# Gram products of a delta-rule attention: two batches in one matmul of 64 columns by 128, and the key block copied in four pieces

## The chip, the cores and the metric

The kernel runs on one core of one Trainium2 chip. A core has engines with queues of their own, in order: TensorE (PE; its weight loads are listed apart as PEld), VectorE (DVE), ScalarE (ACT), GpSimd (POOL) and SyncE (SP), which here only issues transfers. They wait for each other by semaphores. The metric is the device time of one execution in microseconds; the time before is the median of three executions.

## The reference

The input goes through three layers: a delta-rule attention (4 batches, 8 heads, 768 positions, 48 dimensions), a mixture of experts over the 3072 tokens, and a second, soft mixture. The change is in the first:

```python
k_n = k / (np.linalg.norm(k, axis=-1, keepdims=True) + 1e-06)
state = np.zeros((B, H, D, D), dtype=np.float32)
for t in range(S):
    kt, vt, bt = (k_n[:, :, t], v[:, :, t], beta[:, :, t, None])
    y[:, :, t] = np.einsum('bhd,bhde->bhe', q[:, :, t], state)
    v_old = np.einsum('bhde,bhd->bhe', state, kt)
    state = state + bt[:, :, :, None] * np.einsum('bhd,bhe->bhde', kt, vt - v_old)
```

## The kernel before

The 768 positions are cut into 24 steps of 32 positions, and four steps make a slab, of which there are six. Within a step the recurrence is solved with small matrices: the products of the 32 keys with each other (the Gram block K, 32 by 32 for each batch and head), those of the keys with the 32 queries (A, of which only the strictly later queries count), and a triangular inverse T made from K. All of a step's units lie on 128 partitions: partition 32b + i is batch b, position i; the eight heads lie along the free dimension.

`G(t, hh, lo, hi)` (line 188) computes the Gram products of step t for one head of each pair (hh is 0 or 1; p counts the four pairs). For each p and each batch b, one matmul takes the 32 keys as stationary operand (48 rows by 32 columns) and the 32 keys and 32 queries, or one of both (lo, hi), as the moving one. The output of batch b goes to partitions 32b to 32b + 31, so the four batches use four different groups of 32 columns of the array. That is 16 matmuls per call. Each of the two values of hh has one PSUM bank, Gp[0] or Gp[1] (tiles g).

`E(t, hh, lo, hi)` (line 194) empties the bank. ScalarE copies the K half into the slab's tile GK (line 203). VectorE multiplies the A half by the constant mask am into the tile A (line 208): there A has two places side by side for two neighbouring batches, and the mask is zero in the place of the other one. Two neighbouring batches then go through one matmul of 64 rows where A is used (`AU`, line 412). The next call on the same bank has to wait for both readers.

`main` (line 442) has three parts.

1. The start: eight calls of G and E for the K halves of steps 0 to 3, as soon as the keys land. Then VectorE takes the norms of slab 0 (`norms`, with the transpose of GK, line 223) and builds its inverse in 31 operations (`t_ops`, lines 291 to 323). Behind the fourth and each later one of these stands one call: first the eight A halves of steps 0 to 3, then ten calls of both halves, for steps 4 to 8.
2. The loop over 24 steps. A table ORDER sets the order of a step's parts on all engines: KSa, Ub, V, E1, G0, L, Sb, Ua, AUb, E0, KSb, Sa, QS, Ca, T, AUa, G1. KS (line 358), U (380), Sm (395), QS (367) and AU (412) are the matmuls of the recurrence, for two halves a and b of the heads; ScalarE moves their results on: rs (361), uz and un (382, 383) and sbd (404). G0 and G1 are the calls for step t + 9, so they run in the steps 0 to 14 only, two in each. E0 follows G0 in the same step, E1 follows G1 in the next. T (598) and L (607) begin the expert routing, and in some steps ranks are made and rows sent to the experts' buffer by indirect transfers of GpSimd (716). `advance` spreads VectorE's operations for the next slab's inverse over the step.
3. Behind the loop come the experts and the second mixture. They use neither G nor E.

The keys and queries come from the host turned (48 dimensions on partitions 0 to 47 and 64 to 111 for hh 0 and 1), in the free order batch, pair, position (`layouts`, line 1515; `load_kq`, line 167).

Of the kernel before, what the change touches and what calls it, by code (L numbers as in the profile page):

```python
# [21 lines left out]
NP, NCH, NST, NSL = 4, 12, 24, 6  # L22
# [31 lines left out]
def const_array():  # L54
    a = np.zeros((128, NCONST), np.float32)

    def put(k, v):
        lo, hi = CONST[k]
        a[:, lo:hi] = v

    p = np.arange(128)
    put("idn", np.eye(128))
    i = np.arange(32)[None, :]
    par = p[:, None] // 32 % 2 == np.arange(2)[None, :]
    put("par", par)
    put("lo", np.tril(np.ones((8, 8))).reshape(1, 64))
    put("am", (par[:, :, None] & (i > (p % 32)[:, None])[:, None, :]).reshape(128, 64))
    put("ebase", (np.arange(32) % 8 * ESTR)[None, :])
    put("desc", np.arange(8, 0, -1)[None, :])
    put("tri", p[:, None] < p[None, :])  # L70
    put("iota", np.arange(GT)[None, :])
    put("rep", (p % 32)[:, None] == (p % 32)[None, :])
    put("sel", np.stack([(p % 32) // 4 == p // 32, (p % 32) // 4 == 4 + p // 32], axis=1))
    put("tok", (p // 32 * 768 + p % 32)[:, None] + 32 * np.arange(NST)[None, :])
    g = np.array(GTS)
    put("step", GT * np.arange(NOV)[None, :])
    put("tie", np.arange(1, NE)[None, :] / -16.0)
    put("place", np.arange(1, NE)[None, :])
    put("cap", NG * g[None, :])
    put("gcap", (p // 32)[:, None] * g[None, :])  # L80
    put("grp", (p // 32)[:, None] == np.arange(4)[None, :])
    return a
# [39 lines left out]
class Attention:  # L122
# [5 lines left out]
    def __init__(s, tc, ctx, pctx, kqb, scratch, kq, kz, kv, bt, cst, route):  # L128
        s.tc = tc
        nc = s.nc = tc.nc  # L130
        s.kq, s.kz, s.kv, s.bt = kq, kz, kv, bt
        s.route = route
        e = ctx.enter_context
        s.kvp = e(tc.tile_pool(name="akv", bufs=1))
        s.st = e(tc.tile_pool(name="astat", bufs=1))
        s.wk = e(tc.tile_pool(name="awork", bufs=2))
        s.ps = pctx.enter_context(tc.tile_pool(name="apsum", bufs=1, space=PSUM))
        s.kqb, s.scratch, s.vd = kqb, scratch, {}
        s.kvb = [s.kvp.tile([128, 2, 2, 384], F32, name=f"kv{j}") for j in range(3)]
        s.beta = s.st.tile([128, NSL, 32], F32, name="beta")  # L140
        s.lo, s.am, s.par = cst("lo").rearrange("q (i j) -> q i j", i=8), cst("am").rearrange("q (s i) -> q s i", s=2), cst("par")
        s.zero = s.st.tile([128, 128], F32, name="zero")
        s.mk = s.st.tile([128, 1], F32, name="mk")
        s.Sbd = [[s.st.tile([128, 4, 2, 2, 48], F32, name=f"sbd{x}{j}") for j in range(2)] for x in range(2)]
        s.Uz = [s.st.tile([128, 2, 4, 48], F32, name=f"uz{x}") for x in range(2)]
        s.Un = [s.st.tile([128, 4, 48], F32, name=f"un{x}") for x in range(2)]
        s.RS = [s.st.tile([128, 4, 48], F32, name=f"rs{x}") for x in range(2)]
        s.T = s.st.tile([128, 32, 32], F32, name="T")
        bank = lambda name: s.ps.tile([128, 512], F32, name=name)
        s.Gp = [bank(f"g{hh}") for hh in range(2)]  # L150
        s.Sp = s.ps.tile([128, 2, 512], F32, name="sp")
        s.Wp = [bank(f"w{x}") for x in range(2)]
        s.Yp, s.Pp = bank("y"), bank("p")
        s.W = [w[:, 0:192].rearrange("q (h d) -> q h d", h=4) for w in s.Wp]
        s.Y = s.Yp[:, 0:384].rearrange("q (h d) -> q h d", h=8)
        s.kqt, s.kvt, s.GK, s.A, s.GT, s.TD, s.Tt, s.nN, s.nn = ({} for _ in range(9))
        s.spans = list(SPANS[1:])
        s.got = {}
# [8 lines left out]
    def load_kq(s, c, parts=(0, 1), after=None):  # L167
        if c >= NCH:
            return None
        t = s.kqb[c % 7].rearrange("q (s a x) -> q s a x", s=2, a=2)  # L170
        for j in range(2):
            s.kqt[2 * c + j] = t[:, j].rearrange("q a (b p i) -> q a b p i", b=4, p=4)
        for k in parts:
            i = s.load(t[:, :, k], (s.kz, s.kq)[k][c].rearrange("q (s x) -> q s x", s=2), after)
        return i
# [7 lines left out]


    def gram(s, hh):
        return s.Gp[hh][:, 0:256].rearrange("q (p a i) -> q p a i", p=4, a=2)

    def G(s, t, hh, lo=0, hi=2):
        k = s.kqt[t][64 * hh:64 * hh + 48]
        for p in range(4):  # L190
            for b in range(4):
                s.nc.tensor.matmul(s.gram(hh)[32 * b:32 * b + 32, p, lo:hi], k[:, 0, b, p], k[:, lo:hi, b, p], start=True, stop=True)  # L192

    def E(s, t, hh, lo=0, hi=2):
        v = s.nc.vector
        g = s.gram(hh)
        if lo == 0:
            if t // 4 not in s.GK:
                s.GK[t // 4] = s.wk.tile([128, 32, 32], F32, name="GK", bufs=3)
                s.got[t // 4] = 0  # L200
            s.got[t // 4] += 1
            u = (t % 4) * 8 + 4 * hh
            s.nc.scalar.copy(out=s.GK[t // 4][:, u:u + 4], in_=g[:, :, 0])
        if hi == 2:
            if t not in s.A:
                s.A[t] = s.wk.tile([128, 8, 2, 32], F32, name="A", bufs=AH + 3)
            full = [128, 4, 2, 32]
            v.tensor_tensor(out=s.A[t][:, 4 * hh:4 * hh + 4], in0=g[:, :, 1].unsqueeze(2).to_broadcast(full),  # L208
                            in1=s.am.unsqueeze(1).to_broadcast(full), op=ALU.mult)


# [560 lines left out]
class Experts:  # L772
# [140 lines left out]
    def bank(s, name="aux"):  # L913
        return s.ps.tile([128, 512], F32, name="aux", bufs=3) if name == "aux" else s.ps.tile(
            [128, CAP], F32, name=name, **(dict(bufs=2) if name == "h" else {}))
# [286 lines left out]
    def more(s, e, lo, i):  # L1202
# [57 lines left out]
        v.tensor_scalar(out=nm, in0=gm, scalar1=-1.0, scalar2=None, op0=ALU.mult)  # L1260
        sc.activation(out=corr, in_=m, func=AF.Exp, bias=nm)
        sc.activation(out=E, in_=P[0:32, 0:GT], func=AF.Exp, bias=nm)
        v.tensor_reduce(out=rs, in_=E, axis=AX.X, op=ALU.add)
        v.scalar_tensor_tensor(out=sm, in0=sm, scalar=corr, in1=rs, op0=ALU.mult, op1=ALU.add)
        v.tensor_copy(out=m, in_=gm)
        P = aux()
        nc.tensor.transpose(P[0:GT, 0:32], E, idn[0:32, 0:32])
        En = s.wk.tile([GT, 128], F32, name="En")
        v.tensor_copy(out=En[:, 0:32], in_=P[0:GT, 0:32])
# [244 lines left out]

def layouts(q, k, v, beta, moe_w_gate, moe_w_output_gate, moe_w1, moe_w2, moe2_phi, moe2_w1, moe2_w2):
    def turned(a):
        z = np.zeros((NCH, 2, 64, 2, 4, NP, 32), np.float32)
        z[:, :, :48] = a.reshape(4, NP, 2, NCH, 2, 32, 48).transpose(3, 2, 6, 4, 0, 1, 5)
        return z.reshape(NCH, 128, 1024)

    def natural(a):
        return a.reshape(4, 8, NCH, 2, 32, 48).transpose(2, 0, 4, 3, 1, 5).reshape(NCH, 128, 2, 384)

    kq, kz = turned(q), turned(k)

    z = kz.reshape(NCH, 2, 64, 2, 4, NP, 32)
    for i in range(32):
        z[:, i // 16, 48 + i % 16, :, :, :, i] = -1.0
    kv = np.stack([natural(k), natural(v)], axis=3)
    bt = beta.reshape(4, NP, 2, NSL, 4, 32).transpose(0, 4, 2, 1, 3, 5).reshape(128, NSL, 32)  # L1530
    wgo = np.concatenate([moe_w_gate, moe_w_output_gate], axis=1).reshape(3, 128, 16).transpose(1, 0, 2)
    w1 = moe_w1.reshape(8, 3, 128, 8, 128).transpose(0, 3, 2, 1, 4).reshape(8, 8, 128, 384)
    w = np.concatenate([w1, moe_w2.reshape(8, 8, 128, 384)], axis=-1)
    phi = moe2_phi.reshape(3, 128, 32).transpose(1, 0, 2)
    a = moe2_w1.reshape(2, 4, 3, 128, 2, 512).transpose(0, 4, 2, 3, 1, 5).reshape(12, 128, 2048)
    b = moe2_w2.reshape(2, 4, 8, 128, 384).transpose(3, 0, 2, 1, 4).reshape(128, 64, 384)
    w2 = np.zeros((len(PIECES), 128, 2048), np.float32)
    w2[:12] = a
    q = 12
    for lo, n, units in COLS:  # L1540
        for i, k in enumerate(units):
            u = sum(units[:i])
            w2[q, :, :PIECES[q]] = b[:, u:u + k, lo:lo + n].reshape(128, -1)
            q += 1
    return dict(kq=kq, kz=kz, kv=kv, bt=bt, wgo=wgo, w=w, phi=phi, w2=w2, const=const_array())
# [23 lines left out]
```

## Time and profile before

| | us |
|---|---|
| three executions | 605.73 (median), 600.68, 610.77 |
| profiled execution, whole | 608.46 |
| its span, first to last instruction | 606.7 |
| PE busy | 526.8 (87%) |
| DVE busy | 361.7 (60%) |
| ACT busy | 285.9 (47%) |
| POOL busy | 197.8 (33%) |
| G, line 192: PE, busy | 42.9 for 1792 instructions |
| GK copy, line 203: ACT, busy | 13.5 for 48 |

The busy time of an engine is the union of its instructions' times. Matmuls are pipelined, so many short instructions overlap: the 1792 of line 192 have a mean of 243 ns each. Shares over the whole span mix three stages with different limits; the prediction goes by stage. A row of the timeline merges neighbours of one line: start, length, engine, line, operation, names, count, and in brackets how long the engine was idle before it and what ended that.

### The profile page before, as it was taken

The page shows a single profiled execution, that of the slowest core. Times are in us where ns is not written, and L with a number is a line of the kernel's source. Part 1 is how long each engine was busy: PE and PEld are TensorE (multiplying, and loading weights), DVE is VectorE, ACT ScalarE, POOL GpSimd, SP SyncE. Part 2 cuts the span into 40 slices and gives each one's busy share as a digit, 9 for nine tenths or more (in the row PEclk, how much of TensorE's full clock was granted, in tenths as well). Part 3 has the DMA queues.
Part 4 walks back from the last instruction along what each step waited for, and adds up shares of the span by engine and source line. Part 5 has one row for each costly group of instructions (what it writes and reads, how often), then busy time and mean ns, then how long its engine had stood idle before and what let it go on. Part 6 is the DMA issues. An engine that isn't in the chain of part 4 may idle for free.

```text
span 606.7 us, 21501 instructions
## 1 busy us (share of the span) xinstructions
PE 526.8 (87%) x8944; PEld 435.6 (72%) x8945; DVE 361.7 (60%) x1246; ACT 285.9 (47%) x715; POOL 197.8 (33%) x391
## 2 busy tenths in 40 slices
PE   3278869898889768887988999999999999999994
PEld 3255657676666655665887998989999999996353
DVE  1997996597597797002874645555555656554232
ACT  2014446564646646563543544455545555553222
POOL 2111040245354544345303070605343435250400
PEclk9999687787887969797798999999999999998997
DMA  7676884445432346311559877768543544356448
GB/s 227 228 238 181 242 241 152 150 121 174 127 107 72 93 157 210 109 30 66 170 169 377 320 246 233 274 197 296 159 129 99 153 120 129 104 141 241 191 185 244
DMA packets 50347, 107.76 MB, mean 178 GB/s; under 512 B 5928, under 2 KB 28838, under 8 KB 47557
## 3 DMA queue, kind: packets, MB, share of 16 engines
q1 hardware_dynamic: 47189, 100.77, 51.5%
q0 software_dynamic: 2624, 5.16, 2.5%
q8 instruction: 71, 1.16, 0.8%
q10 hardware_dynamic: 432, 0.41, 0.3%
q14 instruction: 31, 0.25, 0.1%
HBM read 86.19 MB, written 20.13 MB: 175 GB/s over the span
## 4 chain that ended last, share of the span: by engine, by line
PE 71%; DVE 12%; issue 5%; ACT 5%; DMA 4%; POOL 1%; another core or an unknown queue 1%; SPq 0%; ACTq 0%; DVEq 0%
PE h L882 6%; PE y L902 6%; PE h L884 6%; PE h L883 6%; PE y L903 5%; PE y L904 5%; PE sp L395 4%; PE y L412 4%; PE w L358 3%; PE w L380 3%; PE g L192 3%; PE y L367 3%; ACT uz L382 2%; PE fa L1358 2%; PE fc L1379 2%
## 5 line engine op out<-in xcount | busy, mean ns | idle before, releaser
L888 DVE SCALAR_TENSOR_TENSOR hTl<-h,hTh 128x224 fp32r<-128x224 f32 (+7 forms) x72 | 38.4, 534 | 84.0 <-ACT hTh L887 83.8
L806 DVE TENSOR_TENSOR w<-kq,w 128x768 fp32r<-128x768 f32 x72 | 71.0, 986 | 15.9 <-ACT w L805 12.0
L882 PE MATMUL h<-xTh,w 128*128 128x224 f32 (+7 forms) x216 | 76.3, 353 | 2.0 <-ACT w L805 1.7
L884 PE MATMUL h<-xTh,w 128*128 128x224 f32 (+7 forms) x216 | 72.8, 337 | 1.5 <-DVE w L806 1.5
L883 PE MATMUL h<-xTl,w 128*128 128x224 f32 (+7 forms) x216 | 72.2, 334 | 1.4 <-DVE xTl L867 1.4
L902 PE MATMUL y<-hTh,w 128*128 128x224 f32 (+7 forms) x216 | 73.4, 340 | 0.0
L903 PE MATMUL y<-hTl,w 128*128 128x224 f32 (+7 forms) x216 | 71.8, 333 | 0.0
L904 PE MATMUL y<-hTh,w 128*128 128x224 f32 (+7 forms) x216 | 71.7, 332 | 0.0
L192 PE MATMUL g<-kq 48*32 48x64 f32 (+1 forms) x1792 | 42.9, 243 | 30.1 <-DVE A L208 15.2
L805 ACT CAST w<-kq 128x768 fp32r<-128x768 f32 x72 | 59.7, 830 | 7.1 <-DMA kq<-in_w_dram 6.9
L887 ACT ACTIVATE hTh<-h 128x224 fp32r<-128x224 f32 (+7 forms) x72 | 34.0, 473 | 61.5 <-PE h L884 61.3
L306 DVE TENSOR_TENSOR Ttmp<-GT,T 128x110 f32<-128x110 f32 (+21 forms) x276 | 60.9, 261 | 0.2
L310 DVE TENSOR_TENSOR T<-T,Ttmp 128x110 f32<-128x110 f32 (+21 forms) x276 | 59.7, 256 | 0.0
L192 PEld LDWEIGHTS g<-kq 48*32 48x32 f32 x1792 | 32.4, 129 | 37.2 <-DVE A L208 18.8
L1117 POOL TENSOR_TENSOR cd<-cd,csm 112x32 f32<-112x32 f32 (+6 forms) x32 | 10.2, 318 | 132.4 <-DVE csm L1115 98.4
L404 ACT COPY sbd<-sp 48x384 f32<-48x384 f32 x92 | 43.7, 475 | 20.1 <-PE sp L395 19.1
L902 PEld LDWEIGHTS y<-hTh,w 128*128 128x128 f32 x216 | 41.7, 193 | 4.9 <-issue 4.4
L882 PEld LDWEIGHTS h<-xTh,w 128*128 128x128 f32 x216 | 41.8, 194 | 4.1 <-ACT w L805 1.8
L382 ACT ACTIVATE uz<-w,csta 128x192 f32<-128x192 f32 x92 | 33.7, 418 | 23.0 <-remote 11.5
L884 PEld LDWEIGHTS h<-xTh,w 128*128 128x128 f32 x216 | 41.9, 194 | 2.7 <-DVE w L806 2.1
L395 PE MATMUL sp<-uz,kv 64*48 64x96 f32 x736 | 32.4, 300 | 13.1 <-ACT uz L382 9.2
L883 PEld LDWEIGHTS h<-xTl,w 128*128 128x128 f32 x216 | 42.0, 195 | 2.0 <-DVE xTl L867 1.6
(289 smaller groups left out, 1034.6 us busy)
## 6 DMA issues: line engine op xcount, KB each, us to landing
kq<-in_w_dram SPq DMA_DIRECT2D x72, 384.0 KB
rb<-in_w_dram SPq DMA_DIRECT2D x12, 1024.0 KB
kv<-in_kv_dram SPq DMA_DIRECT2D x12, 768.0 KB
kq<-in_w_dram SPq DMA_DIRECT2D x7, 1024.0 KB
kq<-in_kz_dram SPq DMA_DIRECT2D x12, 512.0 KB
kq<-in_kq_dram SPq DMA_DIRECT2D x12, 512.0 KB
xb<-none SPq DMA_DIRECT2D x8, 675.5 KB
v<-kv SPq DMA_DIRECT2D x24, 192.0 KB
```

What stands on the lines that cost most here:

```text
L192: s.nc.tensor.matmul(s.gram(hh)[32 * b:32 * b + 32, p, lo:hi], k[:, 0, b, p], k[:, lo:hi, b, p], start=True, stop=True)
L306: v.tensor_tensor(out=t, in0=L[:, j + 1 + a:j + 1 + b, j:j + 1].to_broadcast([128, b - a, j]), in1=T[:, j:j + 1, :j].to_broadcast([128, b ...
L310: v.tensor_tensor(out=x, in0=x, in1=t, op=ALU.add)
L395: nc.tensor.matmul(S[64 * hh:64 * hh + 48, g, :, 2 * x + p], s.kvt[t][64 * g:64 * g + 64, 0, o:o + 48], s.Uz[x][64 * g:64 * g + 64, :, h], ...
L805: s.nc.scalar.copy(out=h, in_=r)
L806: s.nc.vector.tensor_tensor(out=l, in0=r, in1=h.bitcast(F32), op=ALU.subtract)
L882: nc.tensor.matmul(H, a, xh[:, k, lo:hi], start=(k == 0), stop=False)
L883: nc.tensor.matmul(H, a, xl[:, k, lo:hi], start=False, stop=False)
L884: nc.tensor.matmul(H, b, xh[:, k, lo:hi], start=False, stop=(k == 2))
L902: nc.tensor.matmul(Y, a, h, start=(f == 0), stop=False)
L903: nc.tensor.matmul(Y, a, l, start=False, stop=False)
L904: nc.tensor.matmul(Y, b, h, start=False, stop=(f == 7))
```

## The change

Two neighbouring batches go through one matmul: 64 columns of keys as stationary operand (two batches by 32 positions) and 64 keys and 64 queries, or one of both, as the moving one. A call has eight matmuls instead of 16, with outputs on partitions 0 to 63 and 64 to 127. Each result has the products within a batch and those across the two batches; a call fills a whole PSUM bank instead of half of it. For K only the blocks within a batch are wanted, and they lie in different columns for different batches, so ScalarE copies GK in four pieces of 32 partitions instead of one of 128. VectorE's A reads the same number of elements as before: the mask is zero where the batches differ, so it takes both places as they are instead of one block twice. The host's layout of keys and queries is pair, batch, position instead of batch, pair, position; the transfers have the same sizes.

```diff
@@ load_kq
-            s.kqt[2 * c + j] = t[:, j].rearrange("q a (b p i) -> q a b p i", b=4, p=4)
+            s.kqt[2 * c + j] = t[:, j].rearrange("q a (p b i) -> q a b p i", b=4, p=4)
+            s.kqp[2 * c + j] = t[:, j].rearrange("q a (p g x) -> q a p g x", g=2, p=4)
@@ gram, G
-        return s.Gp[hh][:, 0:256].rearrange("q (p a i) -> q p a i", p=4, a=2)
+        return s.Gp[hh].rearrange("q (p a b i) -> q p a b i", p=4, a=2, b=2)
...
-        k = s.kqt[t][64 * hh:64 * hh + 48]
+
+        k = s.kqp[t][64 * hh:64 * hh + 48]
         for p in range(4):
-            for b in range(4):
-                s.nc.tensor.matmul(s.gram(hh)[32 * b:32 * b + 32, p, lo:hi], k[:, 0, b, p], k[:, lo:hi, b, p], start=True, stop=True)
+            for g in range(2):
+                out = s.Gp[hh][64 * g:64 * g + 64].rearrange("q (p a x) -> q p a x", p=4, a=2)[:, p, lo:hi]
+                s.nc.tensor.matmul(out, k[:, 0, p, g], k[:, lo:hi, p, g], start=True, stop=True)
@@ E
-            s.nc.scalar.copy(out=s.GK[t // 4][:, u:u + 4], in_=g[:, :, 0])
+            for b in range(4):
+                r = slice(32 * b, 32 * b + 32)
+                s.nc.scalar.copy(out=s.GK[t // 4][r, u:u + 4], in_=g[r, :, 0, b % 2])
...
-            v.tensor_tensor(out=s.A[t][:, 4 * hh:4 * hh + 4], in0=g[:, :, 1].unsqueeze(2).to_broadcast(full),
+            v.tensor_tensor(out=s.A[t][:, 4 * hh:4 * hh + 4], in0=g[:, :, 1],
                             in1=s.am.unsqueeze(1).to_broadcast(full), op=ALU.mult)
@@ layouts
-        z = np.zeros((NCH, 2, 64, 2, 4, NP, 32), np.float32)
-        z[:, :, :48] = a.reshape(4, NP, 2, NCH, 2, 32, 48).transpose(3, 2, 6, 4, 0, 1, 5)
+        z = np.zeros((NCH, 2, 64, 2, NP, 4, 32), np.float32)
+        z[:, :, :48] = a.reshape(4, NP, 2, NCH, 2, 32, 48).transpose(3, 2, 6, 4, 1, 0, 5)
```

Lines behind E stand six further down afterwards (361 is 367, 404 is 410). The order of the instructions stays on every engine. ScalarE's queue in a loop step, before (GK of g_125 is E1, that of g_124 is E0):

```order
123 L361 COPY rs_121<-w_127 128x192
124 L382 ACTIVATE uz_118<-w_128,csta 128x192 x2
125 L383 COPY un_120<-w_128 128x192
126 L203 COPY GK<-g_125 128x128
127 L614 COPY lg<-p 128x16
128 L404 COPY sbd_115<-sp 48x8x48 x2
129 L382 ACTIVATE uz_117<-w_127,csta 128x192 x2
130 L383 COPY un_119<-w_127 128x192
131 L592 COPY x<-y 128x384
132 L203 COPY GK<-g_124 128x128
133 L361 COPY rs_122<-w_128 128x192
```

The same queue in a step after the change:

```order
136 L367 COPY rs_121<-w_127 128x192
137 L388 ACTIVATE uz_118<-w_128,csta 128x192 x2
138 L389 COPY un_120<-w_128 128x192
139 L209 COPY GK<-g_125 32x128 x4
140 L620 COPY lg<-p 128x16
141 L410 COPY sbd_116<-sp 48x8x48 x2
142 L388 ACTIVATE uz_117<-w_127,csta 128x192 x2
143 L389 COPY un_119<-w_127 128x192
144 L598 COPY x<-y 128x384
145 L209 COPY GK<-g_124 32x128 x4
146 L367 COPY rs_122<-w_128 128x192
```

Each GK copy has become four with the same number of elements per partition, at the same place: before lg and sbd, and before rs. TensorE's queue around the second call of a step (g_125) and the first of the next (g_124), before:

```order
47 L412 MATMUL y<-un_119,A 64x48 x8
48 L192 MATMUL g_125<-kq_73 32x64 x16
49 L358 MATMUL w_127<-sbd_113,kq_69 32x96 x8
50 L380 MATMUL w_128<-rs_122,TD 32x48 x16
51 L192 MATMUL g_124<-kq_73 32x64 x16
52 L607 MATMUL p<-wgo,xT 64x16 x6
53 L395 MATMUL sp<-uz_118,kv_107 48x2x48 x8
```

And after (the matmuls are those of the code; the trace has two instructions for each):

```order
47 L418 MATMUL y<-un_119,A 64x48 x8
48 L196 MATMUL g_125<-kq_73 64x128 x8
49 L364 MATMUL w_127<-sbd_113,kq_69 32x96 x8
50 L386 MATMUL w_128<-rs_122,TD 32x48 x16
51 L196 MATMUL g_124<-kq_73 64x128 x8
52 L613 MATMUL p<-wgo,xT 64x16 x6
53 L401 MATMUL sp<-uz_118,kv_107 48x2x48 x8
```

The calls stand where they stood, between AU and KS and between U and L, with half the matmuls and outputs of 64 partitions by 128 columns.

## Rows read from the trace of the kernel before

**Rows 1.** Stretches: busy us (x instructions) of PE, PEld, DVE, ACT, POOL; PEclk, DMA share, GB/s

```profile
0.00:49.40 49.40, 25.51 (x841) 17.98 (x843) 35.75 (x158) 6.08 (x20) 8.45 (x19) 1.00 0.69 223
49.40:200.00 150.60, 127.63 (x3959) 99.51 (x3962) 117.83 (x539) 83.08 (x253) 50.20 (x138) 0.83 0.52 156
262.00:606.70 344.70, 324.85 (x2726) 280.90 (x2724) 171.91 (x381) 159.81 (x333) 110.86 (x158) 0.95 0.57 188
```

**Rows 2.** Page: busy us, share, instructions; DMA queue: packets, MB, share

```profile
PE 526.8 (87%) x8944; PEld 435.6 (72%) x8945; DVE 361.7 (60%) x1246; ACT 285.9 (47%) x715; POOL 197.8 (33%) x391
...
q8 instruction: 71, 1.16, 0.8%
```

**Rows 3.** Waits of PE, 49.4 to 200 us: for what, us in total, times, longest

```profile
PE g L192 <- issue: 6.4, 9, 3.4
PE w L380 <- issue: 6.4, 6, 1.8
PE sp L395 <- issue: 3.8, 2, 2.2
...
PE sp L395 <- ACT uz L382: 1.5, 6, 0.4
```

**Rows 4.** Timeline of the start

```profile
5.57 3.76 PE L192 MATMUL g<-kq 48*32 48x32 f32 x222 [5.57 <-DMA kq<-in_kz_dram]
...
11.75 1.70 PE L192 MATMUL g<-kq 48*32 48x32 f32 x98 [2.42 <-issue]
...
12.77 1.93 DVE L223 STREAM_TRANSPOSE GT<-GK 128x1024 f32<-128x1024 f32 x1 [11.73 <-ACT GK L203]
...
29.96 0.84 PEld L192 LDWEIGHTS g<-kq 48*32 48x32 f32 x32 [0.53 <-DVE A L208]
...
31.64 0.41 DVE L208 TENSOR_TENSOR A<-g,csta 128x256 f32<-128x256 f32 x1
...
42.13 0.41 DVE L208 TENSOR_TENSOR A<-g,csta 128x256 f32<-128x256 f32 x1
```

**Rows 5.** Timeline of TensorE at the end of a loop step

```profile
124.52 0.87 PE L367 MATMUL y<-sbd,kq 128*32 128x96 f32 x32
...
125.79 0.67 PE L412 MATMUL y<-un,A 64*64 64x48 f32 x16
...
126.39 0.49 PEld L192 LDWEIGHTS g<-kq 48*32 48x32 f32 x32
126.39 0.65 PE L192 MATMUL g<-kq 48*32 48x64 f32 x32
...
126.97 0.54 PE L358 MATMUL w<-sbd,kq 128*32 128x96 f32 x16
```

**Rows 6.** Timeline of ScalarE in the same step

```profile
124.33 0.30 ACT L203 COPY GK<-g 128x128 f32<-128x128 f32 x1
124.49 0.36 ACT L361 COPY rs<-w 128x192 f32<-128x192 f32 x1
124.70 0.97 ACT L404 COPY sbd<-sp 48x384 f32<-48x384 f32 x2
```

**Rows 7.** Groups by shape, 0 to 330 us: busy us, mean ns of one, idle before

```profile
L404 ACT COPY sbd<-sp 48x384 f32<-48x384 f32 x92 | 43.7, 475 | 20.1 <-PE sp L395 19.1
...
L600 ACT COPY xT<-p 128x384 f32<-128x384 f32 x23 | 11.0, 479 | 16.1 <-PE p L598 13.2 <-remote 3.0
```

**Rows 8.** Stretches, columns as in rows 1: between two stops, and an undisturbed step

```profile
80.25:91.54 11.29, 7.94 (x255) 6.24 (x255) 10.41 (x45) 5.62 (x16) 6.12 (x17) 0.80 0.78 230
...
119.50:128.20 8.70, 7.79 (x305) 6.06 (x305) 6.91 (x30) 6.05 (x20) 3.66 (x12) 1.00 0.44 139
```

**Rows 9.** Timeline, while GpSimd issues indirect transfers

```profile
178.27 1.10 POOL L716 DMA_INDIRECT xb<-x,si  x1 [0.55 <-POOL si L715]
...
182.04 0.16 PEld L192 LDWEIGHTS g<-kq 48*32 48x32 f32 x4 [0.47 <-issue]
```

More of the change, by code (lines that the diff above doesn't have):

```diff
@@ L155, in __init__ @@
         s.Y = s.Yp[:, 0:384].rearrange("q (h d) -> q h d", h=8)
+        s.kqp = {}
         s.kqt, s.kvt, s.GK, s.A, s.GT, s.TD, s.Tt, s.nN, s.nn = ({} for _ in range(9))
@@ L1524, in layouts @@
     kq, kz = turned(q), turned(k)
-    z = kz.reshape(NCH, 2, 64, 2, 4, NP, 32)
+    z = kz.reshape(NCH, 2, 64, 2, NP, 4, 32)
     for i in range(32):
```

## The prediction

> **What bounds it now.** I read the table by stage first [rows 1]. Three stretches matter: a start of 49.4 us, in which VectorE builds the first triangular inverse; the steps 0 to 14 of the attention loop, from 49.4 to 200 us, in which Gram products still run; and everything behind, which the change leaves alone. In the start, matmuls are busy for 25.5 us of 49.4 and VectorE for 35.8, nearly all of it from 12.8 us on, so there a Gram call counts only where VectorE waits for it. In the loop, matmuls are busy for 127.6 of 150.6 us and VectorE for 117.8: TensorE is the bound. The table of waits for the same stretch says what its idle time is [rows 3]: 16.6 us of "issue" in 17 waits; the next line, 1.5 us for ScalarE's uz, is small beside it. So TensorE time that is added in the loop lands on the end, and "issue" is the one large thing that could give some back. The granted clock in the loop is 0.83 in the mean: of its two levels the lower one holds for about a third (1 - 2 x 0.17 = 0.66 at the full one).
>
> **What a call costs.** A call G(t, hh) of both halves is 16 matmuls in the code and 32 matmul instructions in the row: an fp32 matmul is two. Four outputs of 32 partitions each go on side by side, so the 32 are eight rounds of four. Two rows price a round by its moving columns [rows 5]: the call with 64 columns takes 0.65 us, L367 with as many instructions and 96 columns 0.87, so 32 columns more cost 0.22. The new call is eight rounds of two with 128 columns: 0.87 + 0.22 = 1.09 us, **0.44 more per call** at the full clock. The load of 64 stationary columns hides below it: L412, eight rounds of two with 64 stationary and 48 moving columns, takes 0.67 in all. That row is the bound below too: were a round no longer than there, a call would cost 0.02 more. Above, if two 64-column outputs did not run side by side, the streams of 0.84 us would take twice as long, about 1.9 us in all; but L412 shows two such outputs overlapping, so I leave that end out.
> The TensorE page of the Trainium skill (TensorE: Matmul & The Clock Gate, "Wait — 56ns, not 53.3ns?") has a floor of about 25 ns from matmul to matmul, however few columns it has. By it the 32 old instructions would need 0.80 us and 16 new ones about the same, and the term would be nil; the row has 32 in 0.65, tail included, so I go by the rows.
>
> **The loop, TensorE: +13.2 us.** 30 of the 56 calls run there (two in each of 15 steps), 30 x 0.44 = 13.2. Nothing covers them: in the row behind the second call, the next step's L358 starts as soon as the call has issued (126.39 to 126.97) [rows 5], while its operand, sbd, was done at 125.67 [rows 6].
>
> **The loop, ScalarE: +1.5 us (0 to 7).** One copy of 128 partitions becomes four of 32. A copy's time follows its free size, not its partitions: 384 elements take 475 ns on 48 partitions and 479 on 128 [rows 7]. So each of the four costs what the one did, 0.30 us, or, as they overlap, the 0.16 us after which the next one starts behind a GK copy (124.33 to 124.49) [rows 6]. Per call ScalarE gets 3 x 0.16 = 0.48 to 3 x 0.30 = 0.90 us more. Queued behind are rs and the two sbd copies, and L358 waits for the latter. They were done 1.3 us before L358 starts, and L358 itself comes 0.44 later, so even 0.90 fits. The other call's copies stand ahead of lg, whose matmuls come 0.44 later as well. What hides them is this slack; where it is missing, 0.90 - 0.44 per call at half the calls is 7 us. VectorE's A waits for the last copy and comes up to 0.9 us later, but it works up to nine steps ahead. I take 1.5.
>
> **The start, first eight calls: +2.2 us (1.4 to 3.1).** Here the loads of one call of 64 columns take 0.84 us (29.96) against 0.49 in the loop (126.39) [rows 4, 5]: the lower of the two levels, 1.2 GHz, though the table prints 1.00 for this stretch. The first eight calls (k half only) begin at 5.57, seven of them take 3.8 us in all, and VectorE's transpose waits for the eighth copy until 12.77 [rows 4]. After the change each has 64 columns in eight rounds, as the call at 29.96 has: 1.1 us, then four copies of 0.75 to 1.2 in all, so a bank comes round every 2.0 to 2.4 us. The eighth call starts at 5.57 + 3 x 2.0 + 0.8 and is copied by 14.2, at the upper end by 15.9. Before, the eighth call came after a stop of 2.4 us of "issue" (11.75) [rows 4]; with 8 x 32 = 256 instructions ahead instead of 8 x 64 = 512, that stop falls behind it. That is in these numbers.
>
> **The start, ten calls of both halves: +5 us (2.9 to 7.3).** From 31.64 to 42.13 VectorE does one A every 1.17 us (nine intervals), each with a step of the inverse [rows 4]. At 1.2 GHz the new call takes 2 x 0.86 = 1.7 us to issue and 1.95 in all, then 0.8 to 1.2 of copies and 0.5 of A before its bank is free: 1.7 to 1.85 us per call with two banks. The first A comes 1.1 later and nine intervals take 15.3 to 16.7 us instead of 10.5: 5.9 to 7.3. But TensorE would then run without gaps, and in the loop the full clock returns behind such stretches; at the full clock a call needs 1.2 us, and if that comes after four calls, the loss is about 2.9. I take the middle.
>
> **Given back: instructions.** The page has 17889 instructions of PE and PEld and 71 packets on an instruction queue: one per 252 [rows 2]. From the stop that ends at 80.3 us to the one that ends at 91.5, 510 instructions are recorded, two such blocks [rows 8], and as many lie between the two stops before them: a stop comes where a block has not arrived. A call loses 32 of its 64 instructions (matmuls and loads). The loop has 7921 in 150.6 us [rows 1], 4.9 us for 256; with 960 fewer in 13 us more it is 6.0, so the next block has 1.1 us longer to come. The long ones among the 17 waits, up to 3.4, 1.8 and 2.2 us by line [rows 3], I count as six: six times 0.9 is 5.4, and I take **-5.5 us (0 to -9)**.
> The Runtime page of the Trainium skill (Runtime: NRT & Kernel Launch, "Instruction fetch mechanics") says that fetching is hidden since instructions issue slower than blocks arrive. By it this term is nil and the time 623.5, within the forecast's own spread; the stops at two blocks' distance speak against it.
> The rest of "issue" stands where GpSimd issues its indirect DMAs: at 178 to 184 us instructions come in bursts with 0.5 to 0.6 us between them [rows 9]. Two Gram calls fall there; with half the instructions they lose less: **-1.5 us (0 to -3)**. And the clock: it drops behind stops (0.80 in the stretch between two of them, 1.00 in the step without one [rows 8]). Fewer stops and longer calls leave fewer of them; about 50 us of the loop are at the lower level, and if one drop in six goes, that is some 5 us of work at half the time: **-2.5 us (0 to -8)**.
> VectorE's A reads as many elements, and the loads are as large as before: nothing. The order of the instructions stays.
>
> **Sum.** 13.2 + 1.5 + 2.2 + 5 - 5.5 - 1.5 - 2.5 = +12.4. The profiled execution took 608.5 us (a span of 606.7 and 1.8 around it), 2.7 above the median of the three runs, 605.7; by the median 605.7 + 12.4 = **618 us**. The three runs spread by 10 us, so about 2%, 12 us, is what a measurement can tell from no change, and the forecast lies on that line.
>
> **The rivals.**
> *Costs at their upper ends (0.2).* ScalarE's copies do not overlap and the start stays at 1.2 GHz: 13.2 + 7 + 3.1 + 7.3 - 5.5 - 1.5 - 1 = +22.6, 628 us. For it: the two sbd copies, 0.97 us for two of 475 ns [rows 6, 7], do not overlap. Against: the slack above.
> *Given back in full (0.18).* -9 - 3 - 8 against 13.2 + 1.5 + 2.2 + 5 = 21.9: +2, 608 us, the same. For it: drops of the clock follow stops. Against: their place is chance, and a new wait makes new ones.
> *Columns cost nothing (0.06).* 30 x 0.02, 1.5 for ScalarE and a start of +3.5 (copies alone), less 9.5 given back: -3.9, 602 us, the same. The floor on the TensorE page of the Trainium skill, above, would do this. Against: 96 columns cost more than 64.
> *Supply is the bound (0.06), faster.* If the loop runs at the pace of its instructions throughout, at 4.9 us per 256, 960 fewer are 18.3 us less. With the start at its low end, +4.3, that is -14.0: 592 us. It decides once each call saves over 0.55 us in the loop (12.1 + 4.3 = 16.4, by 30). For it: 16.6 us of stops. Against: 17 waits are fewer than the loop's 31 blocks, and matmuls are busy for 85%.
>
> **How the numbers follow.** The forecast has 0.5 and reaches from 611 to 626; with the rivals, 605 to 631 leaves 2 in 10 out. Slower by over 2% means above 617.8: a little over half of the forecast and all of the first rival, 0.48. Faster means below 593.6: 0.06. Within 2%: 0.46.
>
> **What would show it.** Gram calls in the loop at 1.09 us with 16 instructions; GK copies 0.16 us apart (right) or 0.30 (upper end); VectorE's first transpose at about 14.4 us and the loop's start at about 57; "issue" in the loop near 10 us instead of 16.6; about 64 instruction packets. If a call stays near 0.65, or the loop is shorter than before, I was wrong about the columns; if the loop's start moves by less than 4 us, about the start.

## The result: 1.4% slower, three quarters of the forecast loss

The changed kernel takes **612.9 us** in the median (610.1 to 614.5), beside 603.2 for the kernel before on the same chip: +9.7 us by the medians, where +12.4 was forecast. The ratio is 1.014, 95% interval 1.010 to 1.019, that is +8.6 us. All ratios here leave out executions over 1.5% slower than the fastest of the same kernel, while the medians have them in. The time lies in the range (605 to 631) and below the point, 618. By the bound of 2% that is "the same", the case that had 0.46; the interval leaves nil out all the same, so "a little slower" says it better. Two repeats, each beside the kernel before on a chip of its own, gave 1.0135 and 1.017 (below).

The profiled execution took 612.7 us. By stage, columns as in [rows 1] (stretch: busy us and instructions of PE, PEld, DVE, ACT, POOL; PEclk, DMA share, GB/s):

```profile
0.00:58.98 58.98, 37.90 (x438) 31.19 (x439) 36.68 (x158) 19.79 (x74) 8.56 (x19) 1.00 0.61 191
58.98:205.10 146.12, 131.77 (x3453) 104.06 (x3450) 119.23 (x540) 103.38 (x340) 49.33 (x135) 0.87 0.51 158
```

The start has grown from 49.4 to 59.0 us. The stretch with Gram calls in the loop, 150.6 us in [rows 1], has become *shorter*: its matmuls are busy for 4.1 us more, yet it ends sooner, since TensorE now stands idle for 14.4 us instead of 23.0. What the changed page says of engines and of the instruction queue (q8), and the two groups that answer to lines 192 and 203 of before:

```profile
PE 542.1 (89%) x8048; PEld 453.0 (74%) x8049; DVE 364.1 (60%) x1246; ACT 321.0 (53%) x859; POOL 197.7 (32%) x391
...
q8 instruction: 64, 1.05, 0.7%
...
L196 PE MATMUL g<-kq 48*64 48x128 f32 (+1 forms) x896 | 70.7, 319 | 20.1 <-DVE A L214 13.0
...
L209 ACT COPY GK<-g 32x128 f32<-32x128 f32 x192 | 49.2, 256 | 31.3 <-DVE Ttmp L312 19.5
```

Half the Gram instructions are busy for 70.7 us where twice as many took 42.9. Four times as many copies cost ScalarE 49.2 us where it spent 13.5, since one of 32 partitions takes 256 ns and one of 128 took 281. Packets on the instruction queue went from 71 [rows 2] to 64.

TensorE's waits in the loop stretch (what was waited for: us in total, times, longest):

```profile
PE w L386 <- issue: 2.1, 4, 0.7
PE y L418 <- issue: 1.9, 1, 1.9
PE sp L401 <- ACT uz L388: 1.7, 7, 0.4
PE p L703 <- ACT lg L620: 1.6, 2, 0.9
PE sp L401 <- issue: 1.6, 4, 0.5
...
PE w L364 <- ACT sbd L410: 0.5, 1, 0.5
```

And three lines of the same view of before that [rows 3] does not have:

```profile
PE g L192 <- DVE A L208: 2.2, 3, 1.0
...
PE p L697 <- ACT lg L614: 0.7, 2, 0.4
PE w L358 <- issue: 0.3, 1, 0.3
```

"Issue" adds up to 7.0 us over all lines, where before had 16.9 (16.6 in the three lines of [rows 3] and 0.3 here), and the waits of 3.4 and 2.2 us are gone. The waits for ScalarE add up to 3.8 us (uz, lg and sbd), where before had 2.2 (uz 1.5, lg 0.7).

The start, as a timeline (start, length, engine, line, operation, idle before it and what ended that): the first copies, VectorE's first transpose, then three of the ten calls of both halves, and the loop's first call.

```profile
6.91 8.99 ACT L209 COPY GK<-g 32x128 f32<-32x128 f32 x32 [3.42 <-PE g L196]
...
15.93 1.92 DVE L229 STREAM_TRANSPOSE GT<-GK 128x1024 f32<-128x1024 f32 x1 [14.89 <-ACT GK L209]
...
36.77 1.06 ACT L209 COPY GK<-g 32x128 f32<-32x128 f32 x4 [0.32 <-PE g L196]
...
36.96 3.35 PE L196 MATMUL g<-kq 48*64 48x128 f32 x32 [0.24 <-DVE A L214]
...
38.98 1.06 ACT L209 COPY GK<-g 32x128 f32<-32x128 f32 x4 [1.15 <-PE g L196]
...
40.07 0.42 DVE L214 TENSOR_TENSOR A<-g,csta 128x256 f32<-128x256 f32 x1 [1.02 <-ACT GK L209]
...
40.55 3.35 PE L196 MATMUL g<-kq 48*64 48x128 f32 x32 [0.24 <-DVE A L214]
...
58.99 1.09 PE L196 MATMUL g<-kq 48*64 48x128 f32 x16
```

The copies of the first eight calls run on without a gap (8.99 us for 32), so there ScalarE sets the pace. In the ten calls TensorE does a pair in 3.35 us, 1.67 us per call, against 1.09 for the same 16 instructions in the loop (last row). Within a call a round of two instructions starts every 0.21 us there and every 0.11 us in the loop: the lower level of the clock. A pair comes round every 3.59 us (36.96 to 40.55), and VectorE, which hardly waited at this place before (once, 0.29 us), waits for GK ahead of A.

**The same table three times.** One profile of each kernel could mislead here, since executions of one kernel differ by some 5 us around their median. So both were profiled in three sessions, the second and third on two different chips. The first profile of before, at 608.5 us, is itself some 5 us above the medians. All numbers are us. "Start" ends where the loop's first Gram call starts, "loop" where the last Gram instruction starts, the rest is what lies behind; PEclk, idle time of TensorE and issue are those of the loop stretch.

| | first transpose | start | loop | rest | PEclk | PE idle | issue |
|---|---|---|---|---|---|---|---|
| before, first | 12.8 | 49.9 | 149.6 | 407.2 | 0.83 | 23.0 | 16.9 |
| after, first | 15.9 | 59.0 | 146.2 | 405.8 | 0.87 | 14.4 | 7.0 |
| before, second | 12.8 | 50.0 | 145.6 | 405.8 | 0.85 | 20.7 | 17.3 |
| after, second | 15.5 | 59.4 | 142.5 | 406.8 | 0.89 | 13.3 | 5.6 |
| before, third | 12.2 | 49.0 | 139.5 | 396.4 | 0.88 | 21.8 | 15.5 |
| after, third | 16.2 | 59.8 | 143.6 | 391.3 | 0.86 | 12.3 | 4.5 |

The start costs 9.1, 9.4 and 10.7 us. The loop differs by -3.4, -3.1 and +4.2, in the mean by -0.8: in these profiles the **start is the loss**, and the loop, in the mean, gives back what it costs.

### The profile page after: what moved, and what is told of

Its sections match the earlier page's. It is cut to its first block, busy times and chain, and to the rows that moved or that the text cites. A ratio compares the mean times of both kernels' runs of the same rounds, so it can differ in the third digit from the quotient of the medians.

```text
span 610.9 us, 19863 instructions
## 1 busy us (share of the span) xinstructions
PE 542.1 (89%) x8048; PEld 453.0 (74%) x8049; DVE 364.1 (60%) x1246; ACT 321.0 (53%) x859; POOL 197.7 (32%) x391
## 4 chain that ended last, share of the span: by engine, by line
PE 72%; DVE 10%; ACT 10%; DMA 3%; issue 3%; another core or an unknown queue 1%; ACTq 0%; DVEq 0%
PE h L888 6%; PE h L890 6%; PE y L908 6%; PE h L889 6%; PE g L196 5%; PE y L909 5%; PE y L910 5%; PE y L418 4%; PE sp L401 4%; PE y L373 4%; PE w L364 3%; ACT uz L388 3%; PE w L386 3%; ACT GK L209 3%; DMA kq<-in_w_dram 2%
## 5 line engine op out<-in xcount | busy, mean ns | idle before, releaser
L196 PE MATMUL g<-kq 48*64 48x128 f32 (+1 forms) x896 | 70.7, 319 | 20.1 <-DVE A L214 13.0
L196 PEld LDWEIGHTS g<-kq 48*64 48x64 f32 x896 | 59.0, 176 | 24.9 <-DVE A L214 15.2
L209 ACT COPY GK<-g 32x128 f32<-32x128 f32 x192 | 49.2, 256 | 31.3 <-DVE Ttmp L312 19.5
L1123 POOL TENSOR_TENSOR cd<-cd,csm 112x32 f32<-112x32 f32 (+6 forms) x32 | 10.7, 334 | 130.3 <-DVE csm L1121 96.3
L975 POOL DMA_INDIRECT cb<-cd,ids x32 | 38.6, 1206 | 11.9 <-POOL cd L1123 11.3
```

What stands on the lines that cost most here:

```text
L196: s.nc.tensor.matmul(out, k[:, 0, p, g], k[:, lo:hi, p, g], start=True, stop=True)
L209: s.nc.scalar.copy(out=s.GK[t // 4][r, u:u + 4], in_=g[r, :, 0, b % 2])
```

## The experiments

All times are medians of executions beside the kernel before on the same chip: 601.8 us in one session (loop alone, copies, columns, both), 602.4 in the second (start alone, late start and the repeats there), 588.9 and 589.8 on two chips on which this kernel is faster.

**The repeats.** Both kernels as they are, for the table above.

> The changed kernel, unchanged, beside the same runs of before as the others: 1.2 to 1.8% slower than before (611 to 613 us where before has 602), a second profile with a first loop call at 59 us and 5 to 9 us of issue in the loop.

> The changed kernel once more beside the same runs of before: 8 to 10 us slower than before (610 to 613 where before has 602); a third profile with 5 to 8 us of issue in the loop and a first loop call at 59 us.

> The kernel before, unchanged, for a second profile: the first one took 608.5 us, while the median of 15 executions is 601.8. Expected: 596 to 606 us, the start as before (first loop call at 49 to 50 us), the loop 3 to 9 us shorter than the 149.5 of the first profile, less time at the lower clock than its 51 us. If the loop is as long and the time falls elsewhere, the stages of the first profile were not typical.

> The kernel before, a third profile: 597 to 608 us, 14 to 19 us of issue in the loop as in the two others, a first loop call at 50 us.

After: 611.0 beside 602.4 (1.0135, interval 1.007 to 1.020) and 598.2 beside 588.9 (1.017, interval 1.013 to 1.021). Before: 603.2 and 586.7, one execution each. The times expected for the third session (610 to 613, 597 to 608) were missed, since they came from chips on which both kernels are slower; the difference, +10.0 by the ratio, was met. "Issue" there, 4.5 us, is below the 5 to 8 expected. The third session's loop stretch, first before, then after:

```profile
49.00:188.50 139.50, 117.73 (x3935) 92.55 (x3930) 120.26 (x539) 82.47 (x253) 54.23 (x131) 0.88 0.53 166
```

```profile
59.70:203.30 143.60, 131.35 (x3457) 104.49 (x3450) 120.31 (x540) 103.24 (x340) 48.73 (x137) 0.86 0.53 164
```

Here the clocks are nearly equal (0.88 and 0.86), and matmuls are busy for 13.6 us more, close to the 13.2 of the forecast, though part of it goes with the clock, which is a little lower after. Idle time pays 9.5 us of it. In the first session the clock of before was 0.83 and after's 0.87, and only 4.1 us more are seen.

**Loop alone: the new form in the loop, the old one in the start.**

```diff
+    def wide(s, t):
+        return t >= AH
...
-        k = s.kqt[t][64 * hh:64 * hh + 48]
+        if not s.wide(t):
...
+            return
+        k = s.kqp[t][64 * hh:64 * hh + 48]
```

Where `wide` is false, G has the 16 matmuls of before and E the one copy.

> The eighteen calls of the start in their old form (16 matmuls, one copy), the thirty of the loop in the new one. Before and after, the first call of the loop starts at 49.9 and 59.0 us, and from it to the last call pass 149.1 and 145.2. Theory (fewer instructions give the loop more than the columns cost it): the start is back at 49.9, the loop stays at 144 to 147, the whole is 2 to 5 us faster than before. Rival (the later start gave the loop its time, since transfers were done and blocks of instructions came sooner): the loop takes 155 to 162 us, and the whole is 6 to 13 slower than before.

Measured: 607.3 beside 601.8, 1.009 (interval 1.004 to 1.013); the expected gain was a miss. The loop of the profile, 148.9 us, is neither the 144 to 147 expected nor the rival's 155 to 162.

> The run with the loop alone in the new form, once more, for its size: first time 607.3 (median of 10, from 602.0 to 612.4) against 601.8. Start alone was 610.3 against 602.4 (+7.9), the changed kernel 611.0 against 602.4 (+8.6). If loop and start add up, the loop's new form costs about 1 us: 602 to 604 here, and the first value was a chance high. If it stays at 606 to 608 (+4 to +6), the loop costs more with the old start than with the new one.

Again, on another chip: 601.7 beside 588.9, +12.8 by the medians; the ratio is 1.014 (interval 1.008 to 1.020). So the new form in the loop is no gain: +5.2 and +8.1 by the ratios. "Issue" in the loop was 6.1 and 6.2 us in the two profiles, as with the whole change. The second one's stretch, its longest stop and its wait for uz:

```profile
49.40:194.00 144.60, 130.87 (x3453) 103.73 (x3450) 120.92 (x540) 103.09 (x340) 51.61 (x135) 0.87 0.51 161
```

```profile
PE y L389 <- issue: 2.4, 1, 2.4
PE sp L417 <- ACT uz L404: 2.3, 10, 0.4
```

**Start alone: `wide` turned round (`t < AH`).**

> The eighteen calls of the start in the new form, the thirty of the loop in the old one: the counterpart of the run with the loop alone. So far (medians, all beside runs of before with a median of 601.8): loop alone 607.3 with its start unchanged, changed kernel 612.9 with a start 9.1 us longer. If the parts add up, this one is 9 slower than before, 610 to 612, and loop alone plus start alone is 5.5 + 9 = 14.5, more than the 10 to 11 of the changed kernel. If a later start gives the loop time (transfers done, blocks of instructions in time), it is 4 to 6 slower, 606 to 608, with a first loop call at 58 to 59 us.

Measured: 610.3 beside 602.4, 1.014 (interval 1.009 to 1.020), as much as the whole change beside the same runs. The first transpose is at 15.5 us, the loop's first call at 59.0. Its loop, in the old form, has the old stops (19.2 us of issue in 19 waits, one of 4.0):

```profile
59.00:211.10 152.10, 127.46 (x3931) 98.91 (x3930) 119.72 (x539) 82.85 (x253) 49.56 (x136) 0.81 0.50 154
```

```profile
PE w L402 <- issue: 7.5, 7, 4.0
PE g L201 <- issue: 4.6, 6, 1.9
PE w L380 <- issue: 4.2, 2, 3.8
```

**Copies alone: before, with GK copied in four pieces.**

```diff
-            s.nc.scalar.copy(out=s.GK[t // 4][:, u:u + 4], in_=g[:, :, 0])
+            for b in range(4):
+                r = slice(32 * b, 32 * b + 32)
+                s.nc.scalar.copy(out=s.GK[t // 4][r, u:u + 4], in_=g[r, :, 0])
```

> The kernel before with GK copied in four pieces of 32 partitions, matmuls unchanged. The four took 1.06 us in the changed kernel. Theory: the first eight calls are bound by ScalarE at 1.06 each, so the first transpose starts at about 14.9 instead of 12.8 us; the ten calls lose another 2 to 3 us, the loop begins 4 to 6 us late; in the loop the copies fall into ScalarE's slack, 149 to 152 us. The whole is 4 to 9 slower than before. If the copies are on the loop's path, it takes 7 us or more longer there.

Measured: 610.1 beside 601.8, 1.014 (interval 1.008 to 1.021). In the start, the copies of the first eight calls run without a gap here too:

```profile
5.89 8.64 ACT L205 COPY GK<-g 32x128 f32<-32x128 f32 x32 [2.41 <-PE g L192]
7.00 0.52 PEld L192 LDWEIGHTS g<-kq 48*32 48x32 f32 x32 [0.95 <-ACT GK L205]
```

The transpose comes at 14.6 us and the loop's first call at 53.6, so of the start's loss the copies alone make 3.7 us, and TensorE waits for ScalarE (0.95 us ahead of a call's loads). The loop of the profile is 148.8 us long, "issue" 16.3: 0.8 us shorter than in the first profile of before, 3.2 longer than in the second. The expectation that the copies fall into ScalarE's slack holds only in part, for TensorE waits for lg and sbd:

```profile
PE p L699 <- ACT lg L616: 2.5, 2, 1.3
PE w L360 <- ACT sbd L406: 2.5, 5, 0.8
PE sp L397 <- ACT uz L384: 1.5, 6, 0.4
```

These are 6.5 us of waits for ScalarE in the loop, where the three profiles of before have 2.0 to 2.4 and those of the changed kernel 3.5 to 4.0. With the 3.7 of the start this comes near the whole loss, 8.3 by the medians; but one profile cannot tell it from the spread between profiles.

**Columns alone: before, each of the 16 matmuls streams its moving columns twice** (32 by 128, the same instruction count, one copy; every product is computed twice). The cut shows G alone; the bank is divided to hold both results, GK is copied from the first of the two, and A reads both.

```diff
-                s.nc.tensor.matmul(s.gram(hh)[32 * b:32 * b + 32, p, lo:hi], k[:, 0, b, p], k[:, lo:hi, b, p], start=True, stop=True)
+                s.nc.tensor.matmul(s.gram(hh)[32 * b:32 * b + 32, p, lo:hi], k[:, 0, b, p],
+                                   k[:, lo:hi, b, p].unsqueeze(2).to_broadcast([48, hi - lo, 2, 32]), start=True, stop=True)
```

> The kernel before with every moving column of a Gram call twice: 16 matmuls of 32 by 128 (32 by 64 for one half), so that a call streams as long as the changed one but keeps its 64 instructions; one copy of GK as before. Theory (the gain is in the count): the loop takes 158 to 162 us, 149 plus 13 for the columns less a little; the start, whose copies are single, ends 4 to 7 us later than before; the whole is 13 to 20 slower than before. Rival (longer streams keep the clock up, whatever the count): the loop takes 145 to 150 us and the mean clock in it rises as in the changed kernel, from 0.83 to 0.87.

Measured: 608.9 beside 601.8, 1.014 (interval 1.008 to 1.019); the whole 13 to 20 us slower and the loop of 158 to 162 us were misses, the loop is 147.0, as the rival had it. A call in the loop, TensorE's row:

```profile
126.63 1.08 PE L192 MATMUL g<-kq 48*32 48x128 f32 x32
```

```profile
52.60:199.60 147.00, 131.33 (x3931) 102.31 (x3928) 119.59 (x539) 82.16 (x253) 49.65 (x138) 0.90 0.52 163
```

The call lasts what the changed one does, 1.08 us, with 32 instructions. So the length is the columns' and not the number of instructions. And in this profile the longer calls do not make the loop longer by their 13 us: with as many instructions as before, "issue" is 10.3 us instead of 16.9, and PEclk is 0.90. The start ends 2.7 us later than before (52.6), so the stages of this profile do not show all of the +8.2 us that the ratio has.

**Both: doubled columns and four copies**, that is the changed kernel's work for TensorE and ScalarE with 64 instructions per call.

> As the run with doubled columns, and GK copied in four pieces: TensorE's streams and ScalarE's copies are those of the changed kernel, only the count of instructions is the old one (64 per call instead of 32). Theory: the start ends 9 us later than before, as in the changed kernel, and the loop takes 158 to 163 us; the whole is 17 to 23 slower than before and 10 to 16 slower than the changed kernel. If the count does nothing, it equals the changed kernel.

Measured: 620.2 beside 601.8. Its executions lie far apart (610.4 to 625.7), so no ratio is given. The start is the changed kernel's (first transpose 15.5, loop's first call 58.3); the loop is 148.8 us with 9.4 of "issue". Beside the changed kernel's loops (142.5 to 146.2 with 4.5 to 7.0) half the instructions go with some 2 to 5 us less of stops, in this one profile. The medians would say 9; with such a spread I don't lean on that.

**Late start: before, with 9.7 us of spare transposes ahead of the last operation of the first inverse.** It asks whether a loop that begins later is shorter.

```diff
+            if j == 30:
+                spare = s.wk.tile([128, 32, 32], F32, name="TD")
+                for _ in range(5):
+                    v.transpose(out=spare.rearrange("p u i -> p i u"), in_=s.T)
```

> The kernel before with five transposes of T into a spare tile ahead of the last operation of the first inverse: VectorE is held for 5 x 1.93 = 9.7 us, all else unchanged; nothing is left out. If a later start gives the loop nothing, 611 to 612 (+9.7). If transfers that are done by then give time back, 605 to 608, with fewer and shorter stops of issue in the loop than the 16.9 us of the profile before.

Measured: 611.8 beside 602.4, 1.014 (interval 1.010 to 1.019): +9.4 by the medians and +8.5 by the ratio for 9.7 us. The delay appears as one long wait for TD, and nearly all of it lands on the end:

```profile
PE w L380 <- DVE TD L323: 9.7, 2, 9.1
PE w L380 <- issue: 6.5, 12, 1.4
```

"Issue" adds up to 14.0 us and no stop is longer than 1.7, so the stops are somewhat less and shorter, as the other theory had it, but the time is not.

**Late start and new loop together**, since the two parts of the change had added up to more than the whole.

> Gram calls of the loop in the new form, those of the start in the old one, and 9.7 us of spare transposes ahead of the last operation of the first inverse (the TD transpose of the start moves to about 57 us). It asks whether the new form costs less in a loop that begins as late as it does in the changed kernel. The new loop alone was 5.2 and 8.1 us above before by the ratios of two sessions, a late old loop +8.5, the whole change +8.1 to +10.0. If a late start gives the new loop back what it costs: +8.5 to +11 over before, a ratio of 1.014 to 1.018, at the changed kernel's time. If the two simply add: +14 to +18, a ratio of 1.023 to 1.030, above the changed kernel; then it is the new form of the start itself (its calls, copies or fewer instructions), not its lateness, that the loop of the changed kernel profits from, or the spread between executions.

Measured: 605.8 beside 589.8, 1.027 (interval 1.020 to 1.035): they add. So a later beginning alone does not make the new loop cheaper.

No variant was faster than the kernel before.

## Why the prediction was nearly right, step by step

**What bounds the stages: right.** The start follows VectorE, and a delay of its inverse reaches the end nearly one for one (late start: +9.4 by the medians, +8.5 by the ratio, for 9.7). The loop follows TensorE, with "issue" as the one large reserve. One reading was off: the next line of the view is not uz's 1.5 us but the 2.2 for VectorE's A; little hangs on it, since after the change it is 1.5.

**A call: right.** 0.65 us became 1.09 as worked out [rows 5], and the run with doubled columns (1.08 with 32 instructions) shows that it is the streamed columns. That speaks against pricing this call by the floor of about 25 ns that the Trainium skill has (TensorE: Matmul & The Clock Gate, "Wait — 56ns, not 53.3ns?"): by it, as the prediction worked out, the term would have been nil, and here it is 0.44 us per call. The old call shows that it does not hold here: its 32 instructions go to four groups of columns, and the four of a round start 7 ns apart. The rival "columns cost nothing" falls with that. In the third pair of profiles matmuls are busy for 13.6 us more; the term was 13.2.

**ScalarE in the loop: copies at the upper end, price as forecast.** The four copies take 1.06 us, so they start 0.26 apart and not 0.16. The pair in [rows 6] that overlapped was a GK copy and an rs, from two banks; four copies of one bank did not overlap here, but that the bank is the reason is not shown. TensorE's waits for ScalarE in the loop rose from 2.2, 2.0 and 2.4 us in the three profiles of before to 3.8, 4.0 and 3.5, by about the 1.5 that the prediction took. The rest was hidden, as argued for sbd: the four copies come late, but so does L358. Where the calls stay short (copies alone), L358 does not come later, and the waits for ScalarE are 6.5 us. So the rival that put 7 us here is refuted for the change as a whole, though its premise on the copies was right. With doubled columns the loop is 147.0 us with one copy and 148.8 with four, in single profiles.

**The start: 9.1 to 10.7 us instead of 7.2, the step that failed.** Two choices within given bounds were wrong, both at the same end. The first eight calls: +3.2, +2.7 and +4.0 (12.8 to 15.9 and so on) where I took 2.2, and 3.1 was the upper end; the 15.9 that it had for the eighth copy is what the first profile shows, by the copies' 0.26 us. The rest of the start, put down to the ten calls: +5.9, +6.7 and +6.8 where I took 5. I had let the full clock come back in the middle of them. It didn't: the pairs are 3.59 us apart from first to last, 1.8 per call, as the upper end had it, and matmuls in that stretch are busy for 87% of the time (columns as above):

```profile
36.70:52.20 15.50, 13.43 (x130) 11.81 (x128) 10.39 (x45) 9.24 (x36) 0.00 (x0) 1.00 0.55 172
```

Its loads stay at the longer time (2.95 us for 32, against 0.85 for 16 in the loop) to the end. The loop's first call is at 58.99, forecast about 57.

**Given back: the mechanism right, the size too small.** "Issue" in the loop fell by 9.9, 11.7 and 11.0 us in the three pairs, where both terms on instructions had 7.0 together. That has two causes, which the runs part, as far as one profile each of two of them can: with longer calls alone and the old number of instructions it is 10.3 (columns) and 9.4 (both), with half as many besides it is 4.5 to 7.0 in six profiles of the new form in the loop (three of the whole change, two of the loop alone, one of the loop with a late start). So more than half of the relief goes with the *length*: each block of 256 instructions [rows 2, 8] lasts longer, and the next one, it seems, is there in time. The forecast had worked out both as one time per block, 4.9 to 6.0 us, and then scaled only six of the 17 waits by it. The Runtime page of the Trainium skill (Runtime: NRT & Kernel Launch, "Instruction fetch mechanics") has fetching hidden; stops that fall from 16.9 to 7.0 us when work per instruction grows speak against it here. That instructions arrive late is still inferred from these stops; no row shows a block's arrival.

**The clock: near in the mean, not in each pair.** PEclk rose from 0.83 to 0.87 and from 0.85 to 0.89, and fell from 0.88 to 0.86. With time at the lower level counted as twice 1 - PEclk of the stretch and half of it as lost, that is -6.6, -6.2 and +3.4 us, in the mean -3.1 where -2.5 stood. The sign of the loop in a pair goes with it. With values this far apart, that their mean lies near the forecast is luck.

**The sum.** By the means of three pairs: start +9.7 (7.2), loop -0.8 (5.2), rest -1.9 (nothing). The loop's own terms, as measured, come near that: 13.2 + 1.5 - 10.9 - 3.1 = +0.7. They do not close exactly: busy time rose by 4.1, 4.3 and 13.6 us, each time 2.5 to 3.0 less than 13.2 and the clock's share together, so one of these two is priced too high. Two errors of size, +2.5 and -6, partly cancel, which is luck: the point is 5 us too high, and without the first error it would be 8. The range would have held either way. The loop came out between the forecast and the rival "given back in full", which had 13.2 + 1.5 - 20 = -5.3 there. "Supply is the bound", which made the kernel faster, is refuted by the loop alone, which with the same 960 instructions fewer is slower than before.

**What stays open.** The parts don't add up. By the ratios the start alone costs 8.6 us and the loop alone 5.2 and 8.1, the whole 8.1 to 10.0. The lower ends of the intervals (+5.2 for the start alone, +2.5 for the loop alone in its first session) would add up to the whole, so chance is not ruled out. That a later loop is cheaper is not borne out by either test (late start, and late start with the new loop, +16). In the third session the profiles place it: up to the last Gram call the loop alone is 5.5 us behind the kernel before and the whole 14.9, of which 10.7 are the start, so there the parts nearly add; behind that call, where the change touches nothing, the whole is 5.2 us *shorter* than before and the loop alone 1.1 longer. In the other sessions the new loop itself was the shorter one. The rest of the kernel varied from 391 to 411 us between profiles, and with such a spread one profile of a kind can't tell a cause from chance.

The granted clock of the executions, all of them and not only the profiled ones, goes with the gap. Its mean over the whole kernel (of the executions that the ratios use) is higher after the whole change than in the kernel before beside it, 0.936 to 0.923 and 0.942 to 0.937 in the two repeats; it is lower with the loop alone (0.927 to 0.929, 0.935 to 0.937), the start alone (0.920 to 0.923) and the copies alone (0.921 to 0.929), and the same with the columns alone (0.929). Counted as above, as time times 1 - clock, the whole change loses 7.7 and 2.2 us less to the lower level than before; loop alone (twice), start alone and copies alone lose 1.9, 1.5, 2.3 and 5.5 us more. That is as large as what does not add up. Why the clock holds up better with both parts than with either one no run shows.

## What to carry to other kernels

Count an engine's cost in streamed columns and in elements per partition, not in instructions. Half the matmuls with twice the columns took 1.09 us instead of 0.65, since two of them run side by side where four did, and four copies of a quarter of the partitions took 1.06 us where one copy had taken 0.30. Where TensorE stops for instructions, longer instructions are partly free, and fewer seem to be worth something besides; read "issue" by stage before pricing added work in full. In a start where one engine's chain waits, take the upper ends: here nothing hid the copies, and the clock did not rise though the stretch was busy. When parts do not add up, compare the granted clock over all executions before looking for a cause in one profile.

## What the runs showed of the hardware

- Copies by ScalarE of 32 partitions by 128 elements take 0.26 to 0.27 us each and followed each other without overlap here, where they read one bank (four in 1.06 us, 32 in 8.99), though a GK copy and an rs started 0.16 apart [rows 6].
- TensorE stayed at its lower level through 15.5 us in which matmuls were busy for 87%, while the table of stretches prints 1.00 there; only the instructions tell it (1.67 us a call beside 1.09 in the loop, a round every 0.21 us beside 0.11).
- Stops for "issue" went with how long the instructions last: 16.9 us in a loop stretch with calls of 0.65 us, 10.3 with as many instructions and calls of 1.08, in one profile.
- Matmul instructions to four groups of columns start 7 ns apart within a round (32 of them in 0.65 us).
